# Attention scores over 32 rows of the array, four heads at a time

## The chip, the cores and the metric

The kernel runs on one core of one Trainium2 chip. The metric is device time in microseconds. Before the change it took 1462.01 us, the median of three runs from 1461.06 to 1463.21.

## The reference

A gated mix of sliding-window attention (A) and a ReLU-gated feed-forward layer (B), forward and backward. The outputs are the layer's result and the gradients of seven inputs.

```python
def _A_ref(x, wqkv, wo):
    H = 32; Dh = D // H; W = 256                      # S = 2048, D = 512, Dh = 16
    qkv = (x @ wqkv).reshape(B, S, 3, H, Dh).transpose(2, 0, 3, 1, 4)
    scores = einsum("bhqd,bhkd->bhqk", q, k) * Dh ** -0.5
    mask = (i - j >= 0) & (i - j < W)
    p = softmax(where(mask, scores, -1e9))
    return einsum("bhqk,bhkd->bhqd", p, v) ... @ wo
def _B_ref(x, W_gate, W_up, W_down):                  # F = 1376
    return (relu(x @ W_gate) * (x @ W_up)) @ W_down
g = sigmoid((x * gate_w).sum(-1))
out = g * _A_ref(...) + (1 - g) * _B_ref(...)
_out, _vjp = jax.vjp(_f, ...); _grads = _vjp(grad_out)
```

## The kernel before

The program has three stages. The feed-forward stage (lines 123 to 238) computes layer B and its weight gradients. The attention stage (lines 240 to 421) follows, and the last stage (from line 423) forms the attention weight gradients, the outputs and the gradient of x. Only attention is touched.

Attention goes over four column blocks c of 128 columns, each of which holds eight heads of 16 columns. A block has four stretches.

*Projections* (lines 269 to 301). For four groups of 512 positions PE makes Q, K, V and the upstream gradient dO, transposed: 128 rows are the eight heads' columns, and the free axis is the position. ACT and DVE evacuate them in turn (helper `evac`, lines 75 and 77). Then DMAs on SP and POOL copy each head's 16 rows of K and V into its own slab of KTz and VTz, which are zero in the other 112 rows (lines 289 to 292; the zeros come from lines 250 and 251, once). So a matmul over all 128 rows with head h8's slab gives that head's scores alone.

*Forward rows j* (lines 306 to 352). For each of 16 blocks of 128 queries and each head, PE writes the causal mask into a PSUM bank (L315) and adds up to three score blocks ST (L318); ACT takes exp (L322) into PuT; POOL zeroes the block at the window's far edge (L324, affine select); PE makes dPT from V and dO (L328); DVE multiplies (L331) into PdPT; PE accumulates PuT and PdPT against K, V and a column of ones into BAp (L334, L337). At the row's end ACT evacuates BAp (L340, L341), and DVE and POOL form the outputs and dq (L342 to L350).

*Transposes* (lines 358 to 375) of Q and dO, scaled on DVE and POOL.

*Backward rows kb* (lines 380 to 416). The same for 128 keys and up to three blocks of queries: scores S2 (L390), exp into Pu2 (L393), two selects on POOL for each head (L394 and, for a full row, L397), dP2 (L401), the product PdP2 (L404), and the accumulation into CDp (L407 over Pu2, called C here, and L410 over PdP2, called D).

The order on each engine is made by the tile framework's scheduler when the program is built: it takes the program's operations by readiness and its own costs, so that the written order of the loops is only a start. Each engine then runs its list in order, and waits at an instruction whose operands aren't there. [...]

## Time and profile before

| | us |
|---|---|
| median of the timed runs | 1462.0 |
| span of the profiled execution | 1462.9 |
| attention, first projection to last dk (337.7 to 1141.2) | 803.5 |
| one column block, the second | 200.7 |
| its projections / forward rows / transposes / backward rows | 17.8 / 99.2 / 8.8 / 74.9 |

The profile page belongs to one profiled execution, whose span is its time from the first to the last instruction. Engines are PE (matmuls), PEld (PE's weight loads), DVE, ACT, POOL and SP. An engine's busy share is an average over stages with different limits, so the stretches are read apart, and within one the chain of waits: for each piece of work what released it.

### The profile page before, as it was taken

The numbers are of one execution on the slowest core, as the hardware profiler recorded it, in microseconds if no ns is written. First come the engines' busy times: TensorE is split into PE (matmuls) and PEld (weight loads), VectorE is DVE, ScalarE is ACT, GpSimd is POOL, SyncE is SP. The second block draws the span as 40 slices with busy tenths as digits, with TensorE's granted clock in tenths as the row PEclk, the third lists the DMA queues.
The fourth block names the chain that finished last, engine by engine and source line by source line (L and its number), as shares of the span: only waits on it lengthen the run. The fifth ranks groups of instructions, "written<-read, shape, count | busy, mean of one in ns | idle before, by whom it ended". The sixth has DMA issues, their size and how long they took to land.

```text
span 1462.9 us, 40605 instructions
## 1 busy us (share of the span) xinstructions
PE 1226.7 (84%) x16120; PEld 884.4 (60%) x16120; DVE 806.1 (55%) x1801; ACT 734.5 (50%) x1706; POOL 677.4 (46%) x1894
## 2 busy tenths in 40 slices
PE   1899999996887998877988879988789558799996
PEld 0556656563776876767848768767678223544443
DVE  0534343434777975778947779757789202333332
ACT  0733232333775975776947759767679100311111
POOL 1434252434556863558925568645588203022111
PEclk9999999997998998998989989989989779899999
DMA  9212122123001011001020010110000792455530
GB/s 248 88 65 98 65 77 83 72 74 95 3 3 31 3 31 30 3 3 31 3 59 3 2 31 4 31 31 3 8 25 4 243 329 88 158 165 152 154 109 19
DMA packets 127249, 99.58 MB, mean 68 GB/s; under 512 B 65521, under 2 KB 112178, under 8 KB 127058
## 3 DMA queue, kind: packets, MB, share of 16 engines
q1 hardware_dynamic: 82034, 56.63, 12.8%
q10 hardware_dynamic: 40160, 27.76, 6.6%
q0 software_dynamic: 4864, 12.59, 2.9%
q8 instruction: 126, 2.06, 0.6%
q14 instruction: 65, 0.53, 0.1%
HBM read 52.92 MB, written 35.82 MB: 61 GB/s over the span
## 4 chain that ended last, share of the span: by engine, by line
PE 58%; ACT 12%; POOL 7%; DVE 7%; issue 6%; DMA 5%; ACTq 2%; SPq 1%; DVEq 0%; POOLq 0%
PE wps L227 5%; ACT PuT L322 3%; PE pp L276 3%; POOL PuT L324 3%; PE dPT L328 3%; PE CDp L407 3%; PE dxps L624 3%; DVE PdPT L331 3%; PE dps L234 3%; PE gps L188 3%; PE ups L191 3%; PE BAp L334 3%; PE bps L588 2%; PE dxps L617 2%; PE dxps L620 2%
## 5 line engine op out<-in xcount | busy, mean ns | idle before, releaser
L331 DVE TENSOR_TENSOR PdPT<-PuT,dPT 128x384 bf16<-128x384 bf16 (+2 forms) x512 | 249.0, 522 | 65.1 <-POOL PuT L324 31.3
L322 ACT ACTIVATE PuT<-ST 128x384 bf16<-128x384 f32 (+2 forms) x512 | 230.9, 480 | 87.8 <-PE ST L318 65.8
L324 POOL TENSOR_SCALAR_AFFINE_SELECT PuT<-PuT 128x128 bf16<-128x128 bf16 x448 | 131.7, 300 | 148.3 <-ACT PuT L322 148.0
L318 PE MATMUL ST<-QT,KTz_3258 128*128 128x128 bf16 x1440 | 195.2, 225 | 0.3 <-DMA KTz_3258<-KTn 0.3
L328 PE MATMUL dPT<-dOT,VTz_3259 128*128 128x128 bf16 x1440 | 167.0, 222 | 1.4 <-DMA VTz_3259<-VTn 1.4
L196 POOL TENSOR_TENSOR hT<-rg,upm 128x512 bf16<-128x512 bf16 (+1 forms) x44 | 50.7, 1154 | 194.9 <-DVE upm L194 194.9
L390 PEld LDWEIGHTS <-QT 128*128 128x128 bf16 x1440 | 106.1, 100 | 30.6 <-DVE R_3270 L371 6.5
L318 PEld LDWEIGHTS <-KTz_3258 128*128 128x128 bf16 x1440 | 116.0, 100 | 4.3 <-issue 2.9
L315 PE MATMUL ST<-mbd,ident 128*128 128x128 bf16 x512 | 114.1, 225 | 4.8 <-ACT KV_3269 L75 1.2
L337 PEld LDWEIGHTS <-PdPT 128*128 128x128 bf16 x1440 | 83.7, 98 | 52.9 <-DVE PdPT L331 49.2
L334 PEld LDWEIGHTS <-PuT 128*128 128x128 bf16 x1440 | 72.0, 96 | 54.8 <-POOL PuT L324 52.0
L328 PEld LDWEIGHTS <-VTz_3259 128*128 128x128 bf16 x1440 | 90.7, 97 | 1.9 <-DMA VTz_3259<-VTn 1.4
L401 PEld LDWEIGHTS <-dOT 128*128 128x128 bf16 x1440 | 89.6, 98 | 0.0
L194 DVE SCALAR_TENSOR_TENSOR upm<-rg,ups 128x512 bf16<-128x512 bf16 (+1 forms) x44 | 30.2, 687 | 92.6 <-PE ups L191 57.6
L227 PE MATMUL wps<-dgu_r,x_r 128*128 128x256 bf16 (+1 forms) x704 | 79.2, 270 | 0.0
L188 PE MATMUL gps<-x_T,Wg_sb 128*128 128x512 bf16 (+1 forms) x176 | 47.9, 396 | 30.3 <-DMA x_T<-in_A_x_dram 22.0
L227 PEld LDWEIGHTS <-x_r 128*128 128x128 bf16 x704 | 66.7, 98 | 8.9 <-DVE dgu_r L77 1.2
L617 PE MATMUL dxps<-WgT_sb,dgT_g 128*128 128x512 bf16 (+1 forms) x176 | 67.2, 382 | 0.0
L620 PE MATMUL dxps<-WuT_sb,duT_g 128*128 128x512 bf16 (+1 forms) x176 | 66.7, 379 | 0.0
L601 POOL DMA_DIRECT2D out_dram<-o_sb x16 | 8.7, 542 | 108.4 <-DVE o_sb L599 108.4
L276 PE MATMUL pp<-x_T,wqkv_sb 128*128 128x512 bf16 x192 | 50.0, 415 | 10.3 <-issue 7.1
L207 POOL TENSOR_TENSOR duT<-dh_sb,rg 128x512 bf16<-128x512 bf16 (+1 forms) x44 | 57.3, 1331 | 0.0
(5482 smaller groups left out, 3484.4 us busy)
## 6 DMA issues: line engine op xcount, KB each, us to landing
dqT_g<-dqkv_d SPq DMA_DIRECT2D x8, 768.0 KB, 16.2
hT_d<-hT SPq DMA_DIRECT2D x10, 512.0 KB, 2.6
dgT_d<-dgT SPq DMA_DIRECT2D x10, 512.0 KB, 3.1
duT_d<-duT SPq DMA_DIRECT2D x10, 512.0 KB, 2.9
hT_g<-hT_d SPq DMA_DIRECT2D x8, 640.0 KB, 5.6
dgT_g<-dgT_d ACTq DMA_DIRECT2D x8, 640.0 KB, 4.9
duT_g<-duT_d ACTq DMA_DIRECT2D x8, 640.0 KB, 6.2
dq_r_25107<-dqkv_d ACTq DMA_DIRECT2D x4, 1024.0 KB, 14.9
```

Of the source, the lines that this page charges most:

```text
L227: nc.tensor.matmul(wps[:, 0:2 * fs], lhsT=x_r[:, t, c * P:(c + 1) * P], rhs=dgu_r[:, t, :, :fs], start=(t == 0), stop=(t == NT - 1))
L276: nc.tensor.matmul(pp[:], lhsT=wqkv_sb[:, cd, col0:col0 + P], rhs=x_T[:, cd, ts_], start=(cd == 0), stop=(cd == DC - 1))
L315: nc.tensor.matmul(ST[:, nb - 1, :], lhsT=ident[:], rhs=mbd[:, 0, :], start=True, stop=True, skip_group_check=True)
L318: nc.tensor.matmul(ST[:, i, :], lhsT=KTz[:, h8, kb * P:(kb + 1) * P], rhs=QT[:, j * P:(j + 1) * P], start=False, stop=True, skip_group_che ...
L322: nc.scalar.activation(PuT[:, :nb, :], ST[:, :nb, :], ACT.Exp, scale=scale)
L324: nc.gpsimd.affine_select(out=PuT[:, 0, :], in_=PuT[:, 0, :], compare_op=ALU.is_ge, fill=0.0, base=-1, pattern=[[-1, P]], channel_multipli ...
L328: nc.tensor.matmul(dPT[:, i, :], lhsT=VTz[:, h8, kb * P:(kb + 1) * P], rhs=dOT[:, j * P:(j + 1) * P], start=True, stop=True)
L331: nc.vector.tensor_tensor(out=PdPT[:, :nb, :], in0=PuT[:, :nb, :], in1=dPT[:, :nb, :], op=ALU.mult)
L334: nc.tensor.matmul(Bacc[:, h8, :], lhsT=PuT[:, i, :], rhs=KV1[:, kb, h8, :], start=False, stop=True, skip_group_check=True)
L390: nc.tensor.matmul(S2[:, i, :], lhsT=QT[:, qb * P:(qb + 1) * P], rhs=KTz[:, h8, kb * P:(kb + 1) * P], start=True, stop=True)
L617: nc.tensor.matmul(dxps[:], lhsT=dgT_g[:fs, fc, lsl], rhs=WgT_sb[:fs, fc, :], start=(i == 0), stop=(i == nmm - 1))
L620: nc.tensor.matmul(dxps[:], lhsT=duT_g[:fs, fc, lsl], rhs=WuT_sb[:fs, fc, :], start=(i == 0), stop=(i == nmm - 1))
```

## The change

Instead of a zero-padded copy for each head, there are two copies of K and of V for each column block: Kp and Vp hold the even heads (odd heads' rows zeroed) and the odd heads (even ones zeroed). They are made from the projection's PSUM bank by a multiplication with a mask of ones and zeros, one on ACT and one on DVE. The score and dP matmuls contract over 32 rows, in which one head of the pair is zero, and use the row group r = 0 to 3 of the array where these rows lie. Heads are taken four at a time, 2r + par, in two halves; within a half the matmuls go over the block i outside and the row group inside. ST and dPT (S2 and dP2) share six PSUM banks; PuT and PdPT have eight buffers instead of four. The masks, exps, selects, products and accumulations stay as they were, and so does the number of matmuls. The accumulations and the mask matmuls contract over all 128 rows as before. The cut diff leaves out the dPT, dP2, product and accumulation loops that change in the same way.

```diff
+    emask = cpool.tile([P, 1], F32, name="emask")
+    omask = cpool.tile([P, 1], F32, name="omask")
+    nc.gpsimd.memset(emask[:], 0.0)
+    for i, t in enumerate(range(P - Dh, 0, -Dh)):
+        nc.gpsimd.affine_select(out=emask[:], in_=emask[:], compare_op=ALU.is_ge, fill=float(1 - i % 2),
+                                base=-t, pattern=[[0, 1]], channel_multiplier=1)
+    nc.vector.tensor_scalar(omask[:], emask[:], -1.0, 1.0, op0=ALU.mult, op1=ALU.add)
...
-            KTz = cp.tile([P, HG, S], BF, name="KTz8")
-            VTz = cp.tile([P, HG, S], BF, name="VTz8")
-            nc.vector.memset(KTz[:], 0.0)
-            nc.gpsimd.memset(VTz[:], 0.0)
...
+                Kp = cp.tile([P, 2, S], BF, tag="Kp")
+                Vp = cp.tile([P, 2, S], BF, tag="Vp")
...
-                            nat = KTn if which == 1 else VTn
+                            nat, par = (KTn, Kp) if which == 1 else (VTn, Vp)
                             evac(nat[:, ts_], pp[:])
-                for h8 in range(HG):
-                    hs = slice(h8 * Dh, (h8 + 1) * Dh)
-                    nc.sync.dma_start(KTz[hs, h8, :], KTn[hs, :])
-                    nc.gpsimd.dma_start(VTz[hs, h8, :], VTn[hs, :])
+                            nc.scalar.mul(par[:, 0, ts_], pp[:], emask[:])
+                            nc.vector.tensor_scalar(par[:, 1, ts_], pp[:], omask[:], None, op0=ALU.mult)
...
-                        for h8 in range(HG):
-                            ST = psA.tile([P, 3, P], F32, tag="ST")
-                            nc.tensor.matmul(ST[:, nb - 1, :], lhsT=ident[:], rhs=mbd[:, 0, :], start=True, stop=True,
-                                             skip_group_check=True)
+                        for par in range(2):
+                            heads = [(r, 2 * r + par) for r in range(4)]
+                            rows = [slice(32 * r, 32 * r + 32) for r in range(4)]
+                            STs = [psA.tile([P, 3, P], F32, name="ST", tag="sc", bufs=6) for _ in heads]
+                            for r, h8 in heads:
+                                nc.tensor.matmul(STs[r][:, nb - 1, :], lhsT=ident[:], rhs=mbd[:, 0, :], start=True,
+                                                 stop=True, skip_group_check=True)
                             for i, kb in enumerate(kbs):
-                                nc.tensor.matmul(ST[:, i, :], lhsT=KTz[:, h8, kb * P:(kb + 1) * P],
-                                                 rhs=QT[:, j * P:(j + 1) * P], start=False, stop=True,
-                                                 skip_group_check=True)
...
+                                for r, h8 in heads:
+                                    nc.tensor.matmul(STs[r][:, i, :], lhsT=Kp[rows[r], par, kb * P:(kb + 1) * P],
+                                                     rhs=QT[rows[r], j * P:(j + 1) * P], start=False, stop=True,
+                                                     skip_group_check=True)
...
+                            for r, h8 in heads:
+                                PuT = wk.tile([P, 3, P], BF, tag="PuT", bufs=8)
+                                PuTs.append(PuT)
+                                nc.scalar.activation(PuT[:, :nb, :], STs[r][:, :nb, :], ACT.Exp, scale=scale)
...
+                            dPTs = [psA.tile([P, 3, P], F32, name="dPT", tag="sc", bufs=6) for _ in heads]
...
-                        for h8 in range(HG):
-                            S2 = psB.tile([P, 3, P], F32, tag="S2")
+                        for par in range(2):
+                            heads = [(r, 2 * r + par) for r in range(4)]
+                            rows = [slice(32 * r, 32 * r + 32) for r in range(4)]
+                            S2s = [psB.tile([P, 3, P], F32, name="S2", tag="sc", bufs=6) for _ in heads]
                             for i, qb in enumerate(qbs):
-                                nc.tensor.matmul(S2[:, i, :], lhsT=QT[:, qb * P:(qb + 1) * P],
-                                                 rhs=KTz[:, h8, kb * P:(kb + 1) * P], start=True, stop=True)
...
+                                for r, h8 in heads:
+                                    nc.tensor.matmul(S2s[r][:, i, :], lhsT=QT[rows[r], qb * P:(qb + 1) * P],
+                                                     rhs=Kp[rows[r], par, kb * P:(kb + 1) * P], start=True, stop=True,
+                                                     skip_group_check=True)
...
+                            for r, h8 in heads:
+                                for i, qb in enumerate(qbs):
+                                    nc.tensor.matmul(Cacc[:, h8, :], lhsT=Pu2s[r][:, i, :], rhs=R1[:, qb, h8, :],
+                                                     start=False, stop=True, skip_group_check=True)
+                            for r, h8 in heads:
+                                for i, qb in enumerate(qbs):
+                                    nc.tensor.matmul(Dacc[:, h8, :], lhsT=PdP2s[r][:, i, :], rhs=Qn[:, qb, h8, :],
+                                                     start=False, stop=True, skip_group_check=True)
```

The order that the scheduler makes changes with it. First place: PE in the middle of the backward rows. Before (S2 is L390, C is L407, D is L410; a head's tiles carry numbers that rise by about 20 from head to head, so Pu2_7360 is exp of S2_7356):

```order
L390 MATMUL S2_7436<-KTz8_3258,QT_3265 128x128
L390 LDWEIGHTS QT_3265
L390 MATMUL S2_7456<-KTz8_3258,QT_3265 128x128 [waits Activation_49]
L410 LDWEIGHTS PdP2_7348 [waits DVE_49]
L410 MATMUL CDp_7334<-Qn_3271,PdP2_7348 128x16
L410 LDWEIGHTS PdP2_7348
L410 MATMUL CDp_7334<-Qn_3271,PdP2_7348 128x16
L410 LDWEIGHTS PdP2_7348
L410 MATMUL CDp_7334<-Qn_3271,PdP2_7348 128x16
L407 LDWEIGHTS Pu2_7360 [waits Pool_49]
L407 MATMUL CDp_7334<-R1_3270,Pu2_7360 128x32
```

PE is at the scores of head 7456 when it comes to C of head 7360. After (S2 is L412, C is L440, D is L444; Pu2_7547 is the last head of a half, and S2_7599 the first of the next):

```order
L412 MATMUL S2_7599<-Kp_3284,QT_3280 128x128
L440 LDWEIGHTS Pu2_7547 [waits Pool_49]
L440 MATMUL CDp_7517<-R1_3287,Pu2_7547 128x32
L440 LDWEIGHTS Pu2_7547
L440 MATMUL CDp_7517<-R1_3287,Pu2_7547 128x32
L412 LDWEIGHTS QT_3280
L412 MATMUL S2_7600<-Kp_3284,QT_3280 128x128
L440 LDWEIGHTS Pu2_7547 [waits Pool_49]
L440 MATMUL CDp_7517<-R1_3287,Pu2_7547 128x32
L444 LDWEIGHTS PdP2_7567
L444 MATMUL CDp_7517<-Qn_3288,PdP2_7567 128x16
```

Further on in the same place:

```order
L444 MATMUL CDp_7517<-Qn_3288,PdP2_7569 128x16
L412 LDWEIGHTS QT_3280
L412 MATMUL S2_7602<-Kp_3284,QT_3280 128x128 [waits PE_49]
L412 LDWEIGHTS QT_3280
L412 MATMUL S2_7602<-Kp_3284,QT_3280 128x128
L412 LDWEIGHTS QT_3280
L412 MATMUL S2_7599<-Kp_3284,QT_3280 128x128
```

The third and last score block of S2_7599 now stands behind C of the half's last head, and behind D of two heads (7567, 7569) of the same half. C waits for POOL at that head's first block and again at its third.

Second place: PE in the middle of the forward rows. Before (mask is L315, ST is L318, A is L337):

```order
L315 MATMUL ST_4612<-mbd_70,ident_65 128x128 [waits PE_49]
L318 LDWEIGHTS KTz8_3258
L318 MATMUL ST_4612<-QT_3265,KTz8_3258 128x128
L337 LDWEIGHTS PdPT_4564 [waits DVE_49]
L337 MATMUL BAp_4530<-KV1_3269,PdPT_4564 128x17
L337 LDWEIGHTS PdPT_4564
L337 MATMUL BAp_4530<-KV1_3269,PdPT_4564 128x17
L337 LDWEIGHTS PdPT_4564
L337 MATMUL BAp_4530<-KV1_3269,PdPT_4564 128x17
L318 LDWEIGHTS KTz8_3258
L318 MATMUL ST_4612<-QT_3265,KTz8_3258 128x128
```

After (mask is L321, ST is L325, A is L355; four heads' ST are written in turn):

```order
L325 LDWEIGHTS Kp_3284
L325 MATMUL ST_4723<-QT_3280,Kp_3284 128x128
L325 LDWEIGHTS Kp_3284
L325 MATMUL ST_4724<-QT_3280,Kp_3284 128x128
L325 LDWEIGHTS Kp_3284
L325 MATMUL ST_4721<-QT_3280,Kp_3284 128x128
L325 LDWEIGHTS Kp_3284
L325 MATMUL ST_4722<-QT_3280,Kp_3284 128x128
L325 LDWEIGHTS Kp_3284
L325 MATMUL ST_4723<-QT_3280,Kp_3284 128x128
L355 LDWEIGHTS PdPT_4681 [waits DVE_49]
L355 MATMUL BAp_4547<-KV1_3286,PdPT_4681 128x17
```

The last score blocks of the four heads 4721 to 4724 stand together before A of head 4681, where before a head's own block followed its mask; between them the matmuls change between 32 and 128 rows.

82 lines of the change are left out of this document (46 added, 36 removed).

## The prediction

> **What bounds the kernel now.** I first read how busy the engines are and the chain of work that ended last, from the page.
>
> ```profile
> PE 1226.7 (84%) x16120; PEld 884.4 (60%) x16120; DVE 806.1 (55%) x1801; ACT 734.5 (50%) x1706; POOL 677.4 (46%) x1894
> PE 58%; ACT 12%; POOL 7%; DVE 7%; issue 6%; DMA 5%; ACTq 2%; SPq 1%; DVEq 0%; POOLq 0%
> ```
>
> 84% of PE invites the thought that cheaper score matmuls pay directly. But this is an average, and a busy PE includes the tails of pipelined matmuls. So I cut one of the four column blocks into its stretches: projections, forward pass (rows j), transposes, backward pass (rows kb). Columns are length, then busy time of PE, PEld, DVE, ACT, POOL, granted clock, DMA share and rate.
>
> ```profile
> 540.90:558.70 17.80, 17.40 (x96) 8.43 (x96) 7.04 (x10) 5.95 (x10) 2.03 (x5) 0.90 0.32 71
> 558.70:657.90 99.20, 80.99 (x1568) 70.44 (x1569) 70.33 (x173) 69.67 (x176) 50.82 (x162) 0.95 0.06 11
> 657.90:666.70 8.80, 1.95 (x32) 1.83 (x33) 7.24 (x35) 0.50 (x2) 7.99 (x20) 0.85 0.46 119
> 666.70:741.60 74.90, 70.95 (x1440) 63.44 (x1441) 65.05 (x144) 65.67 (x176) 62.05 (x241) 0.95 0.01 3
> ```
>
> The two passes hold 174 of the block's 200.7 us, and in the backward pass PE, DVE, ACT and POOL are all over 80% busy: nothing has much slack there. The chain of waits in order of time (start, length, what) gives the period of a row and what sets it. Backward pass:
>
> ```profile
> 498.83 0.51 ACT Pu_7274 L393
> ...
> 499.62 0.53 ACT Pu_7294 L393
> ...
> 500.40 0.06 PE CDp L410 x3
> 500.46 0.08 PE CDp L407 x3
> 500.54 0.18 PE dP_7298 L401 x3
> ...
> 503.38 0.51 ACT Pu_7440 L393
> ...
> 507.92 0.51 ACT Pu_7606 L393
> ```
>
> A row takes 4.54 us, and the chain runs mostly along PE, matmul behind matmul: 25 ns for each narrow one (six in 0.14 us), 58 ns for each 128-wide one (three in 0.18). In the forward pass a row takes 6.17 us, and the chain changes engine all the time:
>
> ```profile
> 588.99 0.50 ACT PuT L322
> 589.49 0.06 issue
> 589.55 0.30 POOL PuT L324
> 589.86 0.04 issue
> 589.90 0.24 PE BAp L334 x3
> ...
> 591.03 0.40 ACT PuT L322
> ...
> 597.20 0.40 ACT PuT L322
> ```
>
> So that pass is bound by the latency from exp to select to matmul, with hand-overs of 0.06 us (ACT to POOL) and 0.04 us (POOL to PE), not by the number of matmuls.
>
> **The change on PE: what it removes and adds.** The matmul count stays. The 5,760 score matmuls go from 128 to 32 rows, and neighbours on different row groups may overlap. No such matmul is in this trace. Its price lies between 58 ns (no overlap) and 58/4 = 15 ns (four at once); a narrow matmul with its weight load passes every 25 ns, so I take 28. What is added is a change of the array's shape whenever a 32-row matmul follows a 128-row one or the reverse. Going through the order, attention has 2,896 of these: 22 in a forward row, 23 in a backward one. The trace has one kind of shape change, to the single-column matmul of line 632 (128*1):
>
> ```profile
> 1296.69 0.61 PE L570 MATMUL pt<-ident,dqT_g 128*128 128x128 bf16 x8
> 1297.23 0.38 PE L632 MATMUL dgw_ps<-x_r_25088,dz_bf 128*1 128x512 bf16 x1
> 1297.54 0.40 PE L570 MATMUL pt<-ident,dqT_g 128*128 128x128 bf16 x4
> ...
> 1451.14 0.38 PE L632 MATMUL dgw_ps<-x_r_25088,dz_bf 128*1 128x512 bf16 x1
> 1451.35 0.38 PE L639 MATMUL dgw_ps<-x_r_25088,dz_bf 128*1 128x512 bf16 x1
> ```
>
> Without a change the next 512-wide matmul starts after 0.21 us, with one after 0.31. Of the eight transposes, the last starts at 1296.69 + 0.61 - 0.22 = 1297.08, and L632 follows 0.15 us later where the transposes' own pace is (0.61 - 0.22)/7 = 0.056. Both ways a change costs 0.095 us. I take that as the nearest row; the bounds are 0 (a change of rows may need no pause) and 0.25 (the whole result time of a 128-wide matmul, 0.22, and a hand-over). At 0.095 a backward row is 23 x 0.095 + 48 x 0.028 + 48 x 0.025 = 4.7 us of PE, against 48 x 0.058 + 48 x 0.025 = 4.0 now. PE gains nothing even in sum.
>
> [...]
>
> **The change in the backward order, the largest term.** Before, PE issues the scores of a head three to five heads before it consumes that head. Now heads come in two halves of four, six banks hold both kinds of scores, and in the order the last score block of the next half's first head stands behind L440 of this half's last head, which waits for that head's second select. Thus there is a loop for each half: exp of the first head, eight selects on POOL in a row, L440, the score blocks behind it, exp again. POOL's rows price the middle:
>
> ```profile
> 499.62 0.52 ACT L393 ACTIVATE Pu_7294<-S_7290 128x384 bf16<-128x384 f32 x1
> 500.20 0.29 POOL L394 TENSOR_SCALAR_AFFINE_SELECT Pu_7294<-Pu_7294 128x128 bf16<-128x128 bf16 x1
> 500.45 0.29 POOL L397 TENSOR_SCALAR_AFFINE_SELECT Pu_7294<-Pu_7294 128x128 bf16<-128x128 bf16 x1
> ...
> 501.43 0.29 POOL L397 TENSOR_SCALAR_AFFINE_SELECT Pu_7340<-Pu_7340 128x128 bf16<-128x128 bf16 x1
> ```
>
> Selects follow each other every 0.246 us (five steps from 500.20 to 501.43). The loop: exp 0.51, hand-over 0.06, selects 7 x 0.246 + 0.29 = 2.01, hand-over 0.04: 2.62 us. Then PE. In the stretch shown above, behind the last wait stand seven narrow matmuls (0.18), four score blocks (4 x 0.028 = 0.11), three changes of shape (0.29), then the result (0.22) and its hand-over (0.03): 0.83. In two neighbouring halves there is one change and it comes to about 0.6. With 0.63 a half is 3.25 us and a row 6.5, against 4.54: +1.96. The last two rows need one select a head and the first fills the pipe, so I count 13 of 16 rows: 4 x 13 x 1.96 = **+102 us**. What is late next is everything behind: DVE's product, the D matmuls, the next half's exp; ACT idles while POOL selects, and POOL idles while PE and ACT start the next half.
>
> **Forward pass.** Here a head has one select, and the row's end (lines 348 to 350 of before) shares POOL and DVE:
>
> ```profile
> 580.46 0.38 POOL t_9292 L348
> ...
> 580.90 0.44 POOL t_9292 L349
> ...
> 441.43 0.35 DVE L350 SCALAR_TENSOR_TENSOR dq_st<-t_5558,rinv 128x128 bf16<-128x128 f32 x1 [0.84 <-POOL t_5558 L349]
> 441.70 2.40 DVE L331 TENSOR_TENSOR PdPT<-PuT,dPT 128x384 bf16<-128x384 bf16 x5
> ```
>
> First half: three exps (0.40 + 0.40 + 0.50), hand-over 0.06, select 0.30, hand-over 0.04, three narrow matmuls, one change, five score blocks and the result 0.56: 2.26 us. Second half: exp 0.50, 0.06, select 0.25, t1 0.38 + 0.44, 0.05, dq 0.31 until the next may start, two products at (2.40 - 0.55)/4 = 0.46 and 0.55, 0.05, then matmuls and result 0.58: 3.63. That chain is 5.89, a floor, since waits outside of it add; the other end is today's 6.17 plus 0.2. I take 6.1: 4 x 14 x -0.06 = **-3 us**.
>
> **Head of a block.** The zero-padded copies go away with their DMAs, and two memsets before the first block.
>
> ```profile
> 557.60 4.54 DMA KTz_3258<-KTn
> L75 ACT COPY KV_8723<-pt 128x1024 bf16<-128x1024 bf16 x2 | 2.0, 1064 | 0.3 <-PE pt L299 0.3
> L75 ACT CAST KTn<-pp 128x512 bf16<-128x512 f32 x4 | 2.3, 587 | 7.0 <-DMA dqkv_d<-dv_st 3.6 <-PE pp L276 3.4
> L77 DVE CAST VTn<-pp 128x512 bf16<-128x512 f32 x4 | 2.8, 692 | 5.4 <-PE pp L276 5.4
> L250 DVE MEMSET KTz_3258<- x1: 6885/6885/6885, 340.1 to 340.1; 128x8192 uint32 x1
> ```
>
> The transfer is 4.54 us of the chain, but the two KV1 evacuations on ACT (2.1 us) and the zeroing copy behind them come next, so I count 2 us for three blocks: **-6 us** (ends 0 and -18). In the first block the memsets, which push back evacuations, give **-1**. The added masked evacuations are 8 on ACT and 8 on DVE a block: 8 x 0.59 = 4.7 and 8 x 0.69 = 5.5 us, on top of 5.95 and 7.04 in a stretch of 17.8 whose PE is full. They hide behind the projections; without that cover they would cost up to 20 us over the four blocks. The seven mask selects at the start lie in POOL's idle time.
>
> Sum: +102 - 3 - 6 - 1 = +92 on the profiled span of 1462.9, hence **1555 us**; that span stands 0.9 above the median of the timed runs (1462.0), within their spread.
>
> **Rivals.** First, every change of shape is a full drain, 0.25 us. Then PE itself is the bound: backward 23 x 0.25 + 2.54 = 8.3 us a row, forward 22 x 0.25 + 8 x 0.058 + 2.54 = 8.5; (8.3 - 4.54) x 52 + (8.5 - 6.17) x 56 - 7 = +319, **1780 us**. For it: there are 2,896 changes. Against: line 632's row. At 0.15 a half grows by 0.1 and PE's own sum nears the loop: about 1620. Second, row groups do not overlap: a score block at 0.058 makes a half longer by 0.15 us; 6.8 and 6.5 a row give 118 + 18 - 7 = +129, **1590**. It is on my side of the sign. Third, changes are free: the PE pieces shrink by 0.1 to 0.3, rows are 6.1 and 5.8, 81 - 20 - 7 = +54, **1515**. Fourth, **faster**: PE's queue gets the next half's scores out before the last select is done, so the loop never closes and the busiest engine decides: ACT in a backward row, 65.67/16 = 4.1 us, DVE in a forward one, 70.33/16 = 4.4. That gives -0.44 x 52 - 1.77 x 56 - 7 = -129, **1335**. It decides if the third score block of a half's first head stands before the wait; the order has it behind in most halves.
>
> **How the numbers follow.** The forecast, with or without overlap of the row groups (1520 to 1640), 0.60; full or near-full drain 0.17; free changes 0.15; faster 0.07; within 0.2% (3 us, about what a measurement of this kernel can tell from no change) 0.01, since all these cases lie far from zero. The likeliest time is 1555. The range goes from 1495, under the free changes, to 1690, a change at about 0.18 us; outside lie the fast case and the upper half of the drain. A lower clock belongs in it too: at 0.85, as in the transposes' stretch, the 0.63 us of a half would grow by 0.07, some 8 us. Faster 0.07, same 0.01, slower 0.92.
>
> **What would show it.** Backward rows 6.5 us apart, with POOL's eight selects in one run, then a gap of about 1.2 us on POOL until the next exp; ACT waiting for PE's L412; L440 waiting for POOL L423; forward rows near 6.1; no DMA at a block's head; after a change from L444 to L412 a pause of 0.1 us. Backward rows at or under 4.5 us, or POOL busy without gaps, would make the prediction wrong; rows of 8 with PE never waiting would be the drain.

## The result and the profile after

The changed kernel takes 1694.22 us (median, 1693.51 to 1695.22), the kernel before 1461.71 beside it: 1.159 times as long, 95% interval 1.157 to 1.160, or +232.5 us. The forecast was 1555, the range 1495 to 1690.

From the page of the changed kernel: busy time of the engines, the granted clock in 40 slices, and the chain that ended last.

```profile
PE 1536.9 (91%) x16062; PEld 906.5 (54%) x16120; DVE 821.0 (49%) x1833; ACT 736.1 (43%) x1738; POOL 652.1 (39%) x1869
PEclk8999999975555575555575555575555558899999
PE 82%; DMA 5%; DVE 4%; ACT 3%; issue 2%; ACTq 2%; POOL 1%; SPq 1%; POOLq 0%; DVEq 0%
```

PE's share of the chain went from 58% to 82%, and the clock row has four plateaus of 5, one for each column block: in attention PE ran at half clock. Before, that row had stayed between 7 and 9:

```profile
PEclk9999999997998998998989989989989779899999
```

Here are pieces of a forward and of a backward pass of the second block (columns as in the prediction's table of stretches: the clock stands ahead of the DMA share).

```profile
622.00:735.00 113.00, 112.38 (x1513) 65.91 (x1513) 68.52 (x165) 62.68 (x164) 49.79 (x157) 0.50 0.01 2
757.00:850.00 93.00, 92.97 (x1230) 58.44 (x1229) 55.06 (x117) 53.67 (x143) 51.65 (x202) 0.50 0.01 2
```

PE is now busy for 112.38 of 113.00 us and for 92.97 of 93.00: it waits for nobody, and it does so at a clock of 0.50, where both passes of before had 0.95. The row's end on ACT (L340 before, L359 now) and the last addition of a backward row on DVE (L415, L449) give the pace, as first and last start of sixteen. Before:

```profile
L340 ACT COPY BA<-BAp x16: 378/384/387, 569.5 to 657.8; 128x264 f32<-128x264 f32 x16
L415 DVE TENSOR_TENSOR dk_st<-CDp,Csb x16: 292/292/293, 676.8 to 741.3; 128x128 bf16<-128x128 f32 x16
```

After:

```profile
L359 ACT COPY BA<-BAp x16: 377/395/397, 622.2 to 735.5; 128x264 f32<-128x264 f32 x16
L449 DVE TENSOR_TENSOR dk_st<-CDp,Csb x16: 284/292/292, 754.7 to 856.4; 128x128 bf16<-128x128 f32 x16
...
L281 PE MATMUL pp<-x_T,wqkv_sb x46: 379/379/631, 596.7 to 612.0; 128*128 128x512 bf16 x46
```

Mean steps (a fifteenth, the shorter rows at the ends included) went from 5.89 to 7.55 us forward and from 4.30 to 6.78 backward: 60 x 1.66 = +100 and 60 x 2.48 = +149. The last line is the block's first projection, at 596.7: the first forward row ended 622.2 - 596.7 = 25.5 us behind it, where before it was 569.5 - 540.9 = 28.6; 4 x -3.1 = -12. The sum, +237, is the +232.5 within 2%.

In the chain of waits a piece of a forward row of the changed kernel looks like this (start, length, what):

```profile
640.71 0.23 PE BAp L355 x9
640.94 0.22 PE ST L325 x2
641.16 0.22 PE dPT L340 x8
```

Where the chain had gone round exp, select and matmul, there is PE alone.

### The profile page after: what moved, and what is told of

Its sections match the earlier page's. It is cut to its first block, busy times and chain, and to the rows that moved or that the text cites. A ratio compares the mean times of both kernels' runs of the same rounds, so it can differ in the third digit from the quotient of the medians.

```text
span 1692.7 us, 40948 instructions
## 1 busy us (share of the span) xinstructions
PE 1536.9 (91%) x16062; PEld 906.5 (54%) x16120; DVE 821.0 (49%) x1833; ACT 736.1 (43%) x1738; POOL 652.1 (39%) x1869
## 4 chain that ended last, share of the span: by engine, by line
PE 82%; DMA 5%; DVE 4%; ACT 3%; issue 2%; ACTq 2%; POOL 1%; SPq 1%; POOLq 0%; DVEq 0%
PE ST L325 9%; PE S L412 9%; PE dP L429 8%; PE dPT L340 6%; PE CDp L440 5%; PE wps L234 4%; PE CDp L444 4%; PE ST L321 4%; PE BAp L351 4%; PE BAp L355 4%; PE pp L281 3%; PE gps L195 2%; PE dps L241 2%; PE ups L198 2%; PE dxps L654 2%
## 5 line engine op out<-in xcount | busy, mean ns | idle before, releaser
L436 DVE TENSOR_TENSOR PdP<-Pu,dP 128x384 bf16<-128x384 bf16 (+2 forms) x512 | 248.9, 526 | 178.4 <-POOL Pu L423 72.4
L419 ACT ACTIVATE Pu<-S 128x384 bf16<-128x384 f32 (+2 forms) x512 | 209.1, 474 | 158.3 <-PE S L412 155.6
L420 POOL TENSOR_SCALAR_AFFINE_SELECT Pu<-Pu 128x128 bf16<-128x128 bf16 x512 | 150.1, 295 | 195.0 <-ACT Pu L419 194.0
L412 PE MATMUL S<-Kp,QT 32*128 32x128 bf16 x1440 | 187.2, 292 | 19.0 <-DVE R L390 19.0
L325 PE MATMUL ST<-QT,Kp 32*128 32x128 bf16 x1440 | 193.3, 291 | 0.0
L429 PE MATMUL dP<-Vp,dOT 32*128 32x128 bf16 x1440 | 163.6, 295 | 3.7 <-ACT Pu L419 3.2
L340 PE MATMUL dPT<-dOT,Vp 32*128 32x128 bf16 x1440 | 145.4, 295 | 3.5 <-ACT PuT L332 3.3
L423 POOL TENSOR_SCALAR_AFFINE_SELECT Pu<-Pu 128x128 bf16<-128x128 bf16 x448 | 131.9, 294 | 0.0
L321 PE MATMUL ST<-mbd,ident 128*128 128x128 bf16 x512 | 116.7, 280 | 4.6 <-ACT KV L75 4.6
L444 PE MATMUL CDp<-Qn,PdP 128*128 128x16 bf16 x1440 | 116.8, 179 | 0.0
L440 PE MATMUL CDp<-R,Pu 128*128 128x32 bf16 x1440 | 115.4, 193 | 0.4
L355 PE MATMUL BAp<-KV,PdPT 128*128 128x17 bf16 x1440 | 111.7, 180 | 2.1 <-DVE PdPT L347 1.7
L444 PEld LDWEIGHTS <-PdP 128*128 128x128 bf16 x1440 | 76.4, 107 | 66.8 <-issue 49.5
L440 PEld LDWEIGHTS <-Pu 128*128 128x128 bf16 x1440 | 70.9, 105 | 62.6 <-POOL Pu L420 13.6
L355 PEld LDWEIGHTS <-PdPT 128*128 128x128 bf16 x1440 | 73.7, 107 | 56.9 <-DVE PdPT L347 22.7
L325 PEld LDWEIGHTS <-Kp 32*128 32x128 bf16 x1440 | 69.4, 104 | 52.7 <-issue 21.4
L351 PEld LDWEIGHTS <-PuT 128*128 128x128 bf16 x1440 | 67.1, 108 | 49.9 <-POOL PuT L334 31.5
```

Of the source, the lines that this page charges most:

```text
L325: nc.tensor.matmul(STs[r][:, i, :], lhsT=Kp[rows[r], par, kb * P:(kb + 1) * P], rhs=QT[rows[r], j * P:(j + 1) * P], start=False, stop=True ...
L340: nc.tensor.matmul(dPTs[r][:, i, :], lhsT=Vp[rows[r], par, kb * P:(kb + 1) * P], rhs=dOT[rows[r], j * P:(j + 1) * P], start=True, stop=Tru ...
L351: nc.tensor.matmul(Bacc[:, h8, :], lhsT=PuTs[r][:, i, :], rhs=KV1[:, kb, h8, :], start=False, stop=True, skip_group_check=True)
L355: nc.tensor.matmul(Aacc[:, h8, :], lhsT=PdPTs[r][:, i, :], rhs=KV1[:, kb, h8, 0:17], start=False, stop=True, skip_group_check=True)
L412: nc.tensor.matmul(S2s[r][:, i, :], lhsT=QT[rows[r], qb * P:(qb + 1) * P], rhs=Kp[rows[r], par, kb * P:(kb + 1) * P], start=True, stop=Tru ...
L419: nc.scalar.activation(Pu2[:, :nb, :], S2s[r][:, :nb, :], ACT.Exp, scale=scale)
```

## The experiments

Three theories were set against each other. A: in the changed kernel the array's cells stream for so small a share of the time that the granted clock falls to 0.50, and at that clock PE is the bound. B: the new order lowers the clock. C: the changes of the array's shape are dearer than the 0.1 us of the prediction, whatever the clock.

**The order alone (full128).** The changed kernel with its halves, six shared banks and eight buffers, but scores over all 128 rows.

```diff
-    lhsT=Kp[rows[r], par, kb * P:(kb + 1) * P], rhs=QT[rows[r], j * P:(j + 1) * P]
+    lhsT=KTz[:, h8, kb * P:(kb + 1) * P], rhs=QT[:, j * P:(j + 1) * P]
...
```

The other three score products change alike, and KTz, VTz, their memsets and their DMAs are those of before.

> The changed kernel's loops, halves, six shared banks and eight buffers, but every score product contracts over all 128 rows from zero-padded copies, with their 16 transfers a block; nothing is left out. PE's order differs from the changed kernel's in 2% of the attention matmuls, and no matmul changes the array's shape. Theory A (in the changed kernel the array streams so little that the granted clock falls to 0.50, and PE at half clock is the bound): the clock here is 0.9 or more in both passes and what is left is the price of the order alone: the loop of a half, 2.62 + 0.66 us, so 6.1 to 6.6 us a backward row, about 6.1 forward, 1530 to 1570 us. Theory B (the order, with PE waiting for POOL, lets the clock fall): 0.50 here too, 56 matmuls of 0.107 and 48 of 0.028 make 7.3 us a forward row, about 6.6 backward, and 1640 or more. Theory C (the changes of shape themselves are dearer than 0.1 us, the clock is a bystander): 1530 to 1570 as A, since no change of shape is left; this run doesn't tell it from A, the others do.

Measured: 1548.84 us, ratio 1.058 (1.056 to 1.060). Both passes, by stretches:

```profile
592.00:676.00 84.00, 75.18 (x1452) 65.06 (x1453) 62.39 (x157) 59.26 (x155) 46.53 (x150) 1.00 0.01 3
700.00:775.00 75.00, 69.16 (x1191) 54.37 (x1188) 52.56 (x112) 51.39 (x137) 50.17 (x198) 1.00 0.01 3
```

The clock is 1.00, so the order isn't what lowers it: B falls. The order costs 85 us, nearly all of it backward. The pace, read as above, is 5.98 us forward (before 5.89) and 5.58 backward (before 4.30):

```profile
L363 ACT COPY BA<-BAp x16: 377/402/403, 589.7 to 679.4; 128x264 f32<-128x264 f32 x16
L453 DVE TENSOR_TENSOR dk_st<-CDp,Csb x16: 283/292/292, 698.7 to 782.4; 128x128 bf16<-128x128 f32 x16
```

The chain of waits shows the predicted loop (score blocks S, exp, selects on POOL), and POOL's own rows show how often it closes:

```profile
722.58 0.37 PE S L416 x6
722.97 0.50 ACT Pu L423
...
725.30 0.25 POOL Pu L427
725.55 1.18 issue
```

```profile
723.53 0.29 POOL L424 TENSOR_SCALAR_AFFINE_SELECT Pu<-Pu 128x128 bf16<-128x128 bf16 x1 [1.26 <-ACT Pu L423]
...
726.76 0.29 POOL L424 TENSOR_SCALAR_AFFINE_SELECT Pu<-Pu 128x128 bf16<-128x128 bf16 x1 [1.21 <-ACT Pu L423]
...
730.06 0.29 POOL L424 TENSOR_SCALAR_AFFINE_SELECT Pu<-Pu 128x128 bf16<-128x128 bf16 x1 [1.28 <-ACT Pu L423]
...
735.60 0.29 POOL L424 TENSOR_SCALAR_AFFINE_SELECT Pu<-Pu 128x128 bf16<-128x128 bf16 x1 [1.26 <-ACT Pu L423]
```

These are the selects behind a pause of POOL, and each is the first of a half: eight selects, a pause of some 1.2 us until the next half's exp, eight selects. From one to the next it is 3.23, 3.30 and 5.54 us. Where the loop closes, a half takes what was worked out (2.62 + 0.66 = 3.28). But the last 5.54 us hold two halves without such a pause between them. So of four halves (12.07 us, 6.04 a row) the loop closes in three, and this pattern goes on until 770 us.

**The row tiling alone (rowsalone).** The loops, banks and buffers of before, one head at a time, with the scores over 32 rows.

```diff
+    rw = slice(32 * (h8 // 2), 32 * (h8 // 2) + 32)
-    lhsT=KTz[:, h8, kb * P:(kb + 1) * P], rhs=QT[:, j * P:(j + 1) * P]
+    lhsT=Kp[rw, h8 % 2, kb * P:(kb + 1) * P], rhs=QT[rw, j * P:(j + 1) * P]
```

> The kernel before with its loops, banks and buffers, one head at a time, but scores over 32 rows from the two masked copies; nothing is left out. The three score blocks of a head lie on one row group, so they can't overlap: 0.058 us each at full clock. 2,920 changes of shape, 28 in a forward row and 18 in a backward one. Theory A with activity counted in time (the array streams as long as before): clock about 0.9; forward row 28 x 0.1 + 56 x 0.058 + 48 x 0.025 = 7.2, backward 18 x 0.1 + 48 x 0.058 + 48 x 0.025 = 5.8 us, at most hidden in part: 1520 to 1600 us. Theory A with activity counted in rows of the array (a 32-row matmul is a quarter of one): clock 0.50; forward 28 x 0.1 + 56 x 0.107 + 48 x 0.028 = 10.1, backward 18 x 0.1 + 48 x 0.107 + 48 x 0.028 = 8.3 us: 1462 + 64 x (10.1 - 6.2) + 60 x (8.3 - 4.5) = about 1900, and over 1800 in any case. Theory C (dear changes of shape, 0.25 us): clock 0.9, forward 11, backward 8.5, over 1900 with a clock that stays high.

Measured: 1764.74 us, ratio 1.206 (1.203 to 1.209), and in both passes:

```profile
640.00:780.00 140.00, 140.00 (x1466) 91.50 (x1467) 71.23 (x159) 68.09 (x159) 48.75 (x153) 0.50 0.01 2
806.00:880.00 74.00, 74.00 (x1171) 48.59 (x1165) 55.95 (x111) 54.34 (x136) 51.89 (x195) 0.50 0.01 3
```

The row tiling alone brings the half clock. One head's three score blocks lie on one row group and did not overlap: at this clock three of them (L406) took 0.49 us and one 0.28, so 0.105 each, twice the 0.054 us of a matmul over 128 rows at full clock in the bench. So PE streams as many clock cycles as before; if that time alone set the clock, it would have stayed near the 0.95 of before. By this run the rows count, too. The forward step is (785.3 - 640.8)/15 = 9.63 us (10.1 worked out), the backward one 5.75 where 8.3 was worked out: there the scheduler puts S of one head beside dP of another, on another row group, and the records show such pairs 0.01 us apart (dP at 819.74, S at 819.75). So the backward sum, and with it "over 1800", was too high.

**PE by itself (bench, bench2).** Stretches of matmuls without any wait for other engines, behind the end of the kernel before; each of the two was run once.

```diff
+        full(400)
+        for _ in range(200):
+            for r in range(4):
+                rowm(r)
+        full(200)
+        for _ in range(400):
+            rowm(0)
...
```

Here `full` is a matmul over 128 rows and 128 columns, `rowm(r)` one over the 32 rows of group r.

> The kernel before, and behind its end a row of PE stretches without any wait on other engines (identity times ones; their output isn't used): 400 matmuls over 128 rows and 128 columns; 800 over 32 rows on the four row groups in turn; 200 full; 400 over 32 rows on one group; 200 full; 100 times (four row groups and one full, two changes of shape); 200 full; 800 full ones of 24 columns; 200 full; 24 times (24 on row groups and 24 of 24 columns, as the changed kernel's rows without waits); 200 full. It measures the disputed prices by themselves. At 0.03, 0.058 and 0.1 us for a row-group matmul, a full one and a change: 23, 23, 12, 23, 12, 38, 12, 20, 12, 36 and 12 us, about 220 us on top of 1462. Theory A in rows: the clock falls towards 0.5 in the one-group stretch, in the stretches with changes and in the narrow one, and comes back in each full stretch; the one-group matmuls then take 0.107 us. Theory A in time: the one-group stretch keeps full clock, the narrow and the mixed ones lose it. The form itself: every stretch with 32-row matmuls is at 0.5, the narrow one is not. Theory C: the clock stays high everywhere and the 200 changes take 0.25 us each or more.

Stretches in the order of time: four groups in turn; one group; full; four groups and one full in turn; 24 columns, early and late; 24 row matmuls and 24 of 24 columns in turn.

```profile
1476.00:1496.00 20.00, 11.78 (x770) 10.95 (x759) 0.00 (x0) 0.00 (x0) 0.00 (x0) 1.00 0.02 5
1516.00:1544.00 28.00, 28.00 (x266) 28.00 (x264) 0.00 (x0) 0.00 (x0) 0.00 (x0) 0.50 0.01 1
1548.00:1556.00 8.00, 8.00 (x147) 8.00 (x145) 0.00 (x0) 0.00 (x0) 0.00 (x0) 1.00 0.01 2
1564.00:1600.00 36.00, 36.00 (x405) 17.15 (x404) 0.00 (x0) 0.00 (x0) 0.00 (x0) 0.50 0.01 1
1616.00:1622.00 6.00, 6.00 (x246) 6.00 (x244) 0.00 (x0) 0.00 (x0) 0.00 (x0) 1.00 0.02 5
1628.00:1634.00 6.00, 5.55 (x207) 5.47 (x204) 0.00 (x0) 0.00 (x0) 0.00 (x0) 0.50 0.01 3
1648.40:1679.90 31.50, 29.39 (x1133) 25.43 (x1133) 0.00 (x0) 0.00 (x0) 0.00 (x0) 0.89 0.02 4
```

So the 32-row form does not hold the clock down: with four groups in turn it is 1.00. With one group it fell to 0.50, though PE had no gap at all (28.00 of 28.00 us). The 0.89 of the last line is a mean over 31.50 us; an estimated 6.9 us of them at 0.50 and the rest at 1.00 would give it. The prices, from the times of single pieces (start, length):

```profile
1480.03 1.97 PE L656 MATMUL bk<-bw,ident 32*128 32x128 bf16 x128 [1.67 <-issue]
...
1557.55 0.23 PE L656 MATMUL bk<-bw,ident 32*128 32x128 bf16 x4
1557.72 0.23 PE L651 MATMUL bk<-bw,ident 128*128 128x128 bf16 x1
1557.88 0.23 PE L656 MATMUL bk<-bw,ident 32*128 32x128 bf16 x4
...
1590.42 0.29 PE L656 MATMUL bk<-bw,ident 32*128 32x128 bf16 x4
...
1590.87 0.29 PE L656 MATMUL bk<-bw,ident 32*128 32x128 bf16 x4
```

Four groups in turn pass at (1.97 - 0.22)/127 = 0.014 us each, a quarter of a full one, until PE waits 1.67 us with no releaser in the profile ("issue"); on the mean of the first stretch it is 20.00/770 = 0.026. A cycle of four and one takes 0.33 us at its start, 1.6 us behind a stretch at 1.00, and 0.45 at half clock. Without the two changes it would be 0.054 (8.00/147) + 4 x 0.014 = 0.11, at half clock twice that; so a change costs 0.11 us at either clock. The prediction's 0.095 was near, and C falls.

> The kernel before, and behind its end PE stretches without waits on other engines (their output isn't used), each between 300 full 128-column matmuls that bring the clock back: the exact order of matmuls of two forward rows of the changed kernel (208 matmuls, 44 changes of shape), played four times; the same order with every score over 128 rows; the same pair for two backward rows (192 matmuls, 50 changes); then 600 matmuls over 128 rows of 28 columns, 600 of 36 columns, and 600 of 128 columns over 32 rows on two groups in turn. It gives PE's own time for a row without any engine to wait for, at full clock for as long as that lasts, and at half. Theory A (half clock made PE the bound): a tiled forward row takes 4.6 to 5.4 us while the clock is at 1.0 (22 changes of 0.1, 48 x 0.02 to 0.028, 8 x 0.053, 48 x 0.025), less than the 6.1 that the order needs, and 7.2 to 7.6 us after it has fallen to 0.50, which is the row of the changed kernel; a backward one 4.3 to 5.0 and 6.2 to 6.8; the rows over 128 rows keep the clock at 1.0 and take 4.2 and 3.9 us. Theory C (the changes are dear whatever the clock): a tiled forward row takes over 6.5 us at full clock too. The last three stretches bracket how much of the array has to stream: one in 28 columns 0.43 of full, 36 columns 0.55, two groups in turn 0.5; with the first bench (0.47 kept, 0.37 lost) I expect 28 columns to lose the full clock, 36 and the two groups to keep it.

Measured, in order: tiled forward rows, the same order over 128 rows, tiled backward rows, the same over 128 rows, 28 columns, two groups in turn. The 28 columns kept 1.00, against the expectation. The 36 columns passed 0.025 us apart (128 in 3.35 us, of which 0.22 for the last result), where half clock would give an estimated 0.030 at least (0.105 x 36/128), so they kept the full clock as expected.

```profile
1483.38:1519.58 36.20, 36.20 (x523) 21.69 (x521) 0.00 (x0) 0.00 (x0) 0.00 (x0) 0.50 0.01 2
1554.00:1570.00 16.00, 16.00 (x390) 16.00 (x388) 0.00 (x0) 0.00 (x0) 0.00 (x0) 1.00 0.01 3
1606.00:1648.00 42.00, 42.00 (x595) 26.93 (x593) 0.00 (x0) 0.00 (x0) 0.00 (x0) 0.50 0.01 2
1674.00:1694.00 20.00, 20.00 (x500) 20.00 (x498) 0.00 (x0) 0.00 (x0) 0.00 (x0) 1.00 0.01 3
1716.00:1730.00 14.00, 14.00 (x559) 13.97 (x557) 0.00 (x0) 0.00 (x0) 0.00 (x0) 1.00 0.02 5
1784.00:1796.00 12.00, 12.00 (x438) 12.00 (x432) 0.00 (x0) 0.00 (x0) 0.00 (x0) 1.00 0.02 4
```

The first stretch is five rows long: 7.24 us a row from PE alone at half clock, against a step of 7.55 in the changed kernel, where PE also never waits. The start of the first forward row still ran faster: seven score blocks took 0.35 us, against 0.51 in the stretch at 0.50. Taken as full clock, it gives PE's time there: the piece from a row's first seven score blocks to a later group of five took

```profile
1470.04 0.35 PE L661 MATMUL bk<-bw,ident 32*128 32x128 bf16 x7
...
1473.11 0.49 PE L661 MATMUL bk<-bw,ident 32*128 32x128 bf16 x5
...
1483.38 0.51 PE L661 MATMUL bk<-bw,ident 32*128 32x128 bf16 x7
...
1487.59 0.49 PE L661 MATMUL bk<-bw,ident 32*128 32x128 bf16 x5
```

3.07 us, and 4.21 for the same piece of a later row. So a tiled forward row would cost PE an estimated 7.24 x 3.07/4.21 = 5.3 us at full clock, less than the step of 5.98 that the order takes without tiling. A tiled backward row at half clock costs 96 x 42.00/595 = 6.8 us, the changed kernel's step. A piece of it that took 6.10 us at half clock (1608.77 to 1614.87) took 4.65 at the start (1597.06 to 1601.71), taken as full clock too, so an estimated 5.2 us a row, less than the order's 5.58. The same orders over 128 rows cost PE 104 x 16.00/390 = 4.3 us a forward row and 96 x 20.00/500 = 3.8 a backward one. By these estimates PE would not have been the bound at full clock in either pass. The kernel itself did not run so: its clock was 0.50.

**Filling the array (warm16, fill20, fill12, full128fill20).** Matmuls that add zeros into the accumulating bank make the array stream and change no result. The first try carried less than was meant: the two lines stood behind the loop over the four heads, so there were 4 in a row and not 16, and its expectation belongs to a kernel that wasn't run.

```diff
+                            for _ in range(10):
+                                nc.tensor.matmul(BAp[:], lhsT=ident[:], rhs=zbf[:, 0:400], start=False, stop=True,
+                                                 skip_group_check=True)
...
```

This is fill20, where they stand behind the dP blocks of a half; fill12 has six there, and warm16 had two behind the B (C) matmuls of a half.

> The changed kernel with two more matmuls behind each head's B and each head's C matmuls: identity times zeros over 400 (384) columns, added to the accumulating bank, so that they add nothing to the result and only make the array stream; 16 in a row, 6,400 columns. Nothing is left out. Theory A: the clock rises to 0.8 or more in both passes and the kernel gets faster although PE does more: at full clock the extra matmuls take 16 x 0.167 = 2.7 us a row, of which a part lies in PE's gaps; rows of 6.7 to 7.2 us where the changed kernel has 7.55 and 6.7, and shorter projections; 1560 to 1660 us. Theory C, or a clock that the 32-row form itself holds at half: clock 0.50, extra matmuls 16 x 0.33 = 5.3 us a row, of which at most half lies in gaps: 1850 us or more.

Measured: 1816.15 us. A stretch of its forward pass:

```profile
390.00:490.00 100.00, 99.90 (x1242) 56.82 (x1241) 52.15 (x128) 50.60 (x128) 39.17 (x127) 0.50 0.01 2
```

The clock stayed at 0.50; with so few fillers that tells nothing yet. With 20 a row:

> The changed kernel with ten zero-adding matmuls behind the dP blocks of every half, 20 in a row (identity times zeros, 400 or 384 columns, into the accumulating bank; nothing is added to the result and nothing is left out). The run warm16 had only 4 a row, not the 16 its expectation reckoned with, and its clock stayed at 0.50. Theory A: at full clock 20 x 0.167 = 3.3 us of streaming a row come to 1.6 forward and 1.1 backward: over half of a row of 8 to 9 us, so the clock stays near 1.0 and the rows take 8 to 9.5 us, 1780 to 1900 us in all. If a clock that the 32-row form or the changes of shape hold at half: PE has no gaps there, 20 x 0.333 = 6.7 us come on top of 7.55 and 6.7, and the time is over 2300 us.

Measured: 1818.59 us. The two passes:

```profile
660.00:740.00 80.00, 70.16 (x1128) 45.56 (x1120) 42.92 (x99) 38.32 (x100) 31.07 (x99) 1.00 0.01 2
800.00:870.00 70.00, 61.86 (x1040) 41.06 (x1042) 39.05 (x81) 35.57 (x99) 36.15 (x144) 1.00 0.01 2
```

Five times as many fillers as in warm16, the same time: the clock is back at 1.00, with all the 32-row matmuls in place, and PE has gaps again. The fillers also moved the order, and with it 2,896 changes of shape became 1,132; but a change cost the same 0.11 us at either clock in the bench. The fillers cost more than the clock gave back, so the kernel isn't faster for it.

> The run full128 (order of the changed kernel, scores over 128 rows) with the same 20 fillers a row as fill20; nothing is left out. Both then run near full clock, so the pair prices the row tiling at equal clock, changes of shape and overlap together. Theory A (the tiling costs by the clock alone, and its changes of shape lie in PE's gaps or are paid for by the overlap): within 2% of fill20's 1819 us; PE's own sum is 56 x 0.053 + 48 x 0.025 + 20 x 0.167 = 7.5 us a forward row here and 56 x 0.02 to 0.028, some 10 changes of 0.1, and the same rest in fill20, 7.0 to 7.5. Theory C (changes of shape dear at any clock): this run is faster than fill20 by 50 us or more.

Measured: 1833.77 us, 0.8% above fill20:

```profile
660.00:740.00 80.00, 74.97 (x1099) 57.55 (x1097) 43.12 (x103) 39.37 (x104) 31.16 (x98) 1.00 0.01 2
800.00:870.00 70.00, 68.20 (x989) 52.22 (x988) 36.66 (x76) 34.30 (x93) 34.15 (x136) 0.97 0.01 2
```

At nearly equal clock (0.97 on the mean in both) the row tiling costs nothing that this pair shows; its run is the faster one by 15 us. With 1,132 changes of shape, though, the pair says little of what 2,896 cost at full clock.

> As the run fill20, but six zero-adding matmuls behind the dP blocks of every half, 12 a row instead of 20; nothing is left out. Theory A, from the benches: the array keeps the full clock where its cells stream some 0.47 of the time or more (two or four row groups in turn, 28 columns of 128 rows), and loses it at 0.42 or less. At full clock 12 fillers give 1.6 + 2.0 us of streaming in a forward row of about 8.2, 0.44, and 1.1 + 1.9 in a backward one of 7.8, 0.39: the clock falls, and then PE at half clock needs 7.2 + 12 x 0.333 = 11.2 us a forward row and 6.7 + 12 x 0.32 = 10.5 a backward one, less the changes of shape that the fillers save, about 10 to 11: 2000 to 2200 us, slower than with 20 fillers (1819) although PE does less. If the clock rises step by step with the work, it is 0.7 to 0.9 and the time lies between 1700 and 1850.

Measured: 1842.89 us, slower than with 20 though PE does less, but by far less than theory A's sentence has it. The time and the mean clock, 0.84, lie where the other sentence put them, yet not for its reason: the clock didn't settle between 0.50 and 1.00. Cut at every 10 us, the second block reads 1.00 in eight of the fourteen pieces from 640 to 780 us and 0.83 to 0.97 in the other six, and 0.50 in all thirteen from 780 to 910. The second block's forward and backward pass, and two stretches of the first block's backward pass:

```profile
660.00:740.00 80.00, 71.92 (x1116) 45.40 (x1116) 44.90 (x107) 38.77 (x104) 30.79 (x99) 0.94 0.01 2
800.00:900.00 100.00, 99.33 (x1092) 51.53 (x1090) 44.58 (x95) 42.15 (x115) 42.57 (x168) 0.50 0.01 2
498.00:546.00 48.00, 44.88 (x671) 26.85 (x661) 26.32 (x56) 25.88 (x70) 25.61 (x102) 0.93 0.01 2
546.00:638.00 92.00, 90.64 (x918) 46.02 (x916) 38.14 (x87) 35.05 (x102) 33.61 (x132) 0.50 0.06 13
```

The second block's forward pass keeps 0.94, and its backward pass is at 0.50 from the start. But the first block's backward pass has a mean of 0.93 for 48 us, and only then 0.50 for 92 us. So it isn't the transposes ahead of the pass alone: with 12 fillers a backward row kept nearly the full clock for 48 us and then lost it.

**Parts of the order, and a faster version (bufs8, sixbanks, banks).** Over 128 rows, with the loops of before: eight buffers for the products alone; six shared banks alone; and another way to deal out buffers and banks.

```diff
-                            ST = psA.tile([P, 3, P], F32, tag="ST")
+                            ST = psA.tile([P, 3, P], F32, tag="ST", bufs=4)
...
-                            dPT = psA.tile([P, 3, P], F32, tag="dPT")
+                            dPT = psA.tile([P, 3, P], F32, tag="dPT", bufs=3)
...
-                    nc.sync.dma_start(KTz[hs, h8, :], KTn[hs, :])
+                        nc.sync.dma_start(KTz[hs, h8, ts_], KTn[hs, ts_])
```

The diff is of banks, which also has BAp with one bank, Pu2 and PdP2 with eight buffers and tags of their own, and VTz like KTz. In bufs8 only PuT and PdPT (with Pu2 and PdP2) get bufs=8; in sixbanks ST and dPT, S2 and dP2 get the shared tag with six.

> The kernel before with one part of the change alone: eight buffers instead of four for the two products of a head (PuT and PdPT, forward and backward). Nothing is left out. If the buffers hold back the exps of later heads now and then, the backward row falls from 4.54 to 4.4 and the forward one hardly: about 1450 us (1440 to 1458). If they are free whenever they are wanted: 1462. Either way the buffers are not what made the changed kernel slower.

> The kernel before with another part of the change alone: scores and dP share six banks, head by head, over 128 rows, four buffers; nothing is left out. The run full128 put the price of the new order at 85 us, all of it in the backward pass. If that comes from the halves (eight selects on POOL in a row, then four heads' matmuls), the shared banks alone cost little: 1460 to 1480 us. If the shared banks are a part of it (a score block of a later head waits for a bank that DVE's product frees last), the backward row is 5 us or more and the time 1490 to 1520. I hold the second for likelier, since PE ran three to five heads ahead with banks of its own for the scores.

> A version to beat both: the kernel before, over 128 rows, with the forward pass's eight banks dealt out as four for scores, three for dP and one for the accumulators instead of 3, 3 and 2, eight buffers for the backward products, and the transfers of the zero-padded copies issued by pieces of 512 columns as soon as their projections are evacuated. Nothing is left out. If the forward row is bound by the latency from exp to select to matmul, a fourth score bank lets PE run one head further ahead: the row goes from 6.17 towards DVE's own 4.4 us, I take half way, 5.3: 56 x 0.87 = -49 us; the transfers off the chain 3 x 4.5 = -14; the buffers up to -10: about 1395 us (1370 to 1440). The rival: with one accumulator bank the next row's first B matmuls wait for this row's copies (0.39 + 0.28 us and the zeroing 0.53), 1.2 us a row: 1462 + 64 x (1.2 - 0.87) - 14 = about 1470.

Measured: bufs8 1452.89 us, 0.992 (0.989 to 0.994); sixbanks 1496.63, 1.023 (1.021 to 1.025); banks 1389.55, **0.949** (0.946 to 0.952). So of the order's 85 us the shared banks are 33, the buffers give 11 back, and the halves, if these add, are the rest, 63. In the forward pass of banks, where the clock is 1.00, PE is busy for 69.91 of 76.00 us:

```profile
549.00:625.00 76.00, 69.91 (x1513) 64.33 (x1510) 64.53 (x166) 63.78 (x165) 49.61 (x157) 1.00 0.02 5
```

This is the version that beats both. Its three parts were not run one by one.

## Why the prediction was wrong

*The direction and the order were right.* "+102" for the backward order was +77 by itself (60 x 1.28), and the run with the order alone took 1549 where the forecast for everything was 1555. A half's length was right where the loop closes (3.23 and 3.30 us against 3.25), in part by luck: the forecast counted 0.1 to 0.29 us for changes of shape in a half, and the run with the order alone has none, but scores at 0.058 instead of 0.028 us. How often the loop closes was wrong: in three halves of four, not in each, so a full row rose by 1.50 us (6.04 - 4.54) and not by 1.96. Forward -3 was +5 without the tiling; the head of a block gave 12 instead of 6, although the masked evacuations didn't hide quite: a block's first mask matmul came 19.9 instead of 18.6 us behind its first projection.

*The step that failed is the sentence on the clock*: "A lower clock belongs in it too: at 0.85 [...] some 8 us." The working took the durations of a kernel at 0.95 for one in which most of the streaming was taken away. (The 0.85 was no clock but a mean: the trace of before holds only 0.50 and 1.00.) In the changed kernel the clock was 0.50, in both passes, and that is the other 145 us (1694 - 1549): 60 x (7.55 - 5.98) = 94 forward, 60 x (6.78 - 5.58) = 72 backward, less 12 at the blocks' heads; that is 154, and 9 us of it are not accounted for. The same step hid in "PE gains nothing even in sum": the sum of 4.7 against 4.0 us in a backward row is one for full clock; at half it is the 6.8 us of the bench.

The clue stood in numbers that were at hand. A full matmul passes in 0.054 us (8.00/147 in the bench). By its rows a 32-row one is counted as a quarter of that, 0.0135, and by its columns a narrow one of 25 columns as 25/128, 0.0105. So the shares of the time here are estimates, at full clock:

| cells streaming | forward | backward | clock |
|---|---|---|---|
| before: 56 (48) x 0.054 + 48 x 0.0105, over 6.17 (4.54) | 0.57 | 0.68 | 0.95, 0.95 |
| full128: the same over 5.98 (5.58) | 0.59 | 0.55 | 1.00, 1.00 |
| changed: 8 (0) x 0.054 + 48 x 0.0135 + 48 x 0.0105, over the same | 0.26 | 0.21 | 0.50, 0.50 |
| warm16: 4 fillers of 0.169 (0.162) more, over the same | 0.38 | 0.32 | 0.50 |
| fill12: 12 more, over 8.2 (8.8) | 0.44 | 0.35 | 0.94, 0.50 |
| fill20: 20 more, over 8.8 (7.6) | 0.56 | 0.58 | 1.00, 1.00 |

The steps of full128 and the fill runs are a fifteenth of the time from first to last row end, as above. The 8.8 of fill12 is a step at half clock; in its first block, while the clock was up, backward rows took 7.45 us (503.26, 510.71, 518.15), a share of 0.42. In the benches the full clock was kept by four groups in turn (0.0135/0.026 = 0.52), two groups (0.0135/0.0274 = 0.49) and 28 columns (0.0118/0.025 = 0.47), and lost by 24 columns (0.010/0.0244 = 0.41), four groups and one full with changes (2 x 0.054/0.33 = 0.33) and one group (0.25). The last stretch of the bench, with a mean clock of 0.89, had 576 x (0.0135 + 0.0101)/31.5 = 0.43. One line between 0.41 and 0.47 fits these means. That is a bracket from a few stretches (28 columns ran for 15 us only).

The clock records in the traces of the two kernels, before and changed, tell more. The granted clock has no value in them but 0.50 and 1.00, and each of their 58 stretches of one value, up to the last of each trace, lasts a multiple of 3.41 us, from 1 to 85 of them. Cut at that step, with each matmul counted as 0.054 us x columns/128 x rows/128 in the window in which it starts, the two traces give 908 windows. Behind each of the 338 windows with a share under 0.30 the clock of the next was 0.50; behind each of the 538 with 0.45 or more it was 1.00; and that held whichever clock was granted before (25 of the 338 stood at 1.00, 22 of the 538 at 0.50). The best single line, 0.34, lies under the bracket of the means and is wrong for 7 windows. Counted without the rows the best line is wrong for 74, and by PE's busy time for 296. So in these two traces rows and columns both count. Fill12's backward pass, which stayed at 0.50 once it was there, fits: at half clock its rows get longer and their estimated share smaller (3.1/8.8 = 0.35 against 0.42).

*The rivals.* A wait for the whole result at each change (the full drain, 0.25 us): refuted, 0.11 us in the bench; its 1780 and the upper bound of 1690 came near the measured time for another reason. Row groups that don't overlap: refuted, 0.014 us against 0.054. Free changes: refuted by the same 0.11 us. The fast case: refuted, since the loop does close. *What would show it:* PE never waiting was named as the mark of the drain; it came with steps of 7.55 and 6.78, and only the clock column tells the two apart.

Idle gaps of PE don't explain the lower clock: in the changed kernel PE was busy for 112.38 of 113.00 us at 0.50. Nor does a change of shape look like a wait for results: in the bench a full matmul starts 0.17 us behind the first of four row matmuls whose results take 0.23, a pause, but as far as these ends can be trusted (the profile models them) no wait for their results. Four row groups in turn passed at 0.054/0.014 = 3.9 times the pace of full matmuls within a run of 128, at 128 columns, and at 0.054/0.026 = 2.1 times with the standstills between.

What stays open: how the tiled kernel would run at full clock without fillers, and whether an order with fewer changes of shape would help it at half.

## What to carry to other kernels

Before making matmuls smaller, work out which share of the array's cells will be streaming, and read the granted clock by stages (in the traces of before and after, 1.00 stood behind each of the 538 windows of 3.41 us with a share of 0.45 or more): here a PE that was "busy" with small pieces for 112.38 of 113.00 us had a clock of 0.50, and so became the bound it wasn't. If the matmuls aren't the bound, spare the array's work last: here a fourth score bank, early transfers and more buffers took 5% off, where cheaper matmuls with their order cost 16%. An edit that carries its own loop order is two edits; run the order alone.

## What the runs showed of the hardware

In the traces of the two kernels the granted clock followed the estimated share of cells that stream, rows times columns, in the window of 3.41 us before: behind each of 338 windows under 0.30 it was 0.50, behind each of 538 from 0.45 on it was 1.00. PE's busy time sorts these windows worse (296 of 908 wrong, against 7). In the benches 400 matmuls on one row group brought the clock to 0.50, with PE busy for 28.00 of 28.00 us; the same form was at 1.00 for 12 us on two groups and for 20 us on four. Adding work paid for itself in clock: 20 fillers a row took 1818.59 us, 4 took 1816.15. The fall wasn't at once: 24 columns still had 1.00 at 1616 to 1622 us of the bench and 0.50 from 1628 to 1634. Row groups in turn passed 0.014 us apart, 128 matmuls at a time, and then PE stood still for 1.50 to 2.05 us with no releaser in the profile; what it waited for was not shown.
